# Turning a unit's maxima in the middle of the next burst, with rows that go through memory

## The chip, the cores and the metric

The kernel runs on one core of a Trainium2 chip. The metric is the device time of one execution in microseconds (us). The engines are PE (TensorE: matmuls; the profile lists its weight loads apart, as PEld), DVE (VectorE), ACT (ScalarE), POOL (GpSimd) and SP (SyncE, which issues nearly all DMAs here). Each engine runs its own instructions in order.

## The reference

Input x has 2048 rows (tokens) and 640 columns. The result mixes two branches with one gate per token:

```python
g = sigmoid((x * gate_w).sum(-1, keepdims=True))
a = softmax(q @ k.T * 20**-0.5) @ v     # 32 heads of 20, q, k, v = x @ wqkv
y = Cr @ (x @ Dr.T) - Ci @ (x @ Di.T)   # Fourier transform over hidden and tokens, real part
out = g * (a @ wo) + (1 - g) * y
```

All is in fp32. The softmax needs the maximum of each row of scores; that maximum is what the change is about.

## The kernel before, in words

**Projections.** Ahead of the main loop the kernel projects x to q, k and v (`qk_tile`, `v_pair`) and stores them to memory. Among the last q and k tiles stand ten *segments* (`segment`, `FILL`): in each, some steps of scores for maxima (`s_step`) alternate with the matmuls of one tile of the hidden Fourier transform (`hid_tile`). `FILL[4] = (0, 8, 7, 0)` means: a step and 0 pairs of the tile's matmuls, a step and 8, a step and 7, a step and 0. `HEAD` is the number of segments, `LEAD` the number of score steps done ahead of the loop: 10 x 4 and one more.

**Units and their two kinds of scores.** Attention goes by 32 units (a pair of heads times one half of the query tokens), each of 32 steps. Scores are computed twice. An *m* (`s_mm`, L171) multiplies 128 queries with 512 keys, and DVE reduces the tile to one maximum per query (L173). An *e* (L880) computes transposed scores, keys by queries, and ACT takes the exponential out of PSUM (L886). In the e, two extra rows of the q stack (rows `KROWS` and `KROWS + 1` of each half of the partitions) hold the negated maximum, split into two fp32r parts, and the k stack has ones there: the matmul subtracts the maximum. So all maxima of a unit have to be in these rows before its first e. The m's run `LEAD` steps ahead of the e's.

**From maxima to rows.** `max_nm` (L187) reduces a unit's 64 partial maxima per partition to 16 (2 heads x 8 query tiles), negated: nm, 128 x 16. `max_chain` turns nm with a PE transpose into 16 x 128 in a PSUM bank (L205), splits it on DVE into m1 and m2 (L115, L116), and four DMAs on SP copy them, 8 partitions each, into the four rows of the q stack (L213, L214).

**The main loop.** It is written out by hand as a string per cycle of 4 steps, `ORDER = "emFemFFFFemFeFFmeFFemFFFmmFFmeeB"`: 8 e's, 8 m's, 15 places for fills F (matmuls of the Fourier transform, later of the output projection; L614, L363, L685) and one burst B. From cycle `late` on there are no m's and the string is `LATE`. In a burst, `max_nm` runs first for a unit whose last m is done; then come reads of finished fill tiles (`run_extras`) and two AV steps (`av_step`, L533), each of four fp32 matmuls in the four 32-column quarters of the array, which add exp(scores) @ v; after them `max_chain`. The scores, the turn and the projections take PSUM banks in rotation from five (`bank`); a bank is free when its last reader is done.

**SP's order.** `at_step(i, fn)` puts a DMA into SP's program at the beginning of step i; SP issues in this order as early as what it waits for allows. The rows of a unit are placed two steps behind the turn. On the same queue are the loads of the Fourier matrices (in_cdft), of partial results (a_scr), the stores and loads of the softmax sums (l_scr, r_scr), and the loads of the next pair of heads (qk_scr).

**The lines to follow.** `FILL` and `LEAD` near the top, `s_end`, `max_nm` and `max_chain` (L175 to L219), the loop over `order` that calls `segment` (L438 to L453), and `burst` (L892 to L904).

Of the kernel before, what the change touches and what calls it, by code (L numbers as in the profile page):

```python
# [10 lines left out]
F32 = mybir.dt.float32  # L11
R = mybir.dt.float32r
AF = mybir.ActivationFunctionType
ALU = mybir.AluOpType
AX = mybir.AxisListType
# [3 lines left out]
P = 128  # L19
# [9 lines left out]
KROWS = 3 * DH  # L29
NU = 2 * NP  # L30
# [7 lines left out]
FIRST = {"e": (0, 0, 1, 1), "m": (1, 1, 1, 1)}  # L38


LEAD = 41


FILL = {4: (0, 8, 7, 0)}
HEAD = 10


# [23 lines left out]
def f32(ap):  # L71
    return ap.bitcast(F32)
# [3 lines left out]
def mix_kernel(ctx: ExitStack, tc: tile.TileContext, xa, wqk, wb, cdft, wo, out):  # L76
    nc = tc.nc
    pe, act, dve, pool, sp = nc.tensor, nc.scalar, nc.vector, nc.gpsimd, nc.sync
    ctx.enter_context(tc.manual_schedule())

    def pools(**kw):
        return ctx.enter_context(tc.tile_pool(**kw))

    const = pools(name="const", bufs=1)
    small = pools(name="small", bufs=1)
    work = pools(name="work", bufs=1)
    dram = pools(name="dram", bufs=1, space=DRAM)
# [8 lines left out]
    r_scr = dram.tile([NU, 4, 512], F32, name="r_scr")  # L96
    l_scr = dram.tile([NU, 4, 512], F32, name="l_scr")
    o_scr = dram.tile([D, S], F32, name="o_scr")

    ident = const.tile([P, P], F32, name="ident")  # L100
    make_identity(nc, ident)
# [9 lines left out]
    def split(dst1, dst2, src, e1, e2):  # L111
        if e1 is act:
            act.activation(dst1, src, AF.Copy)  # L113
        else:
            e1.tensor_copy(dst1, src)  # L115
        e2.tensor_tensor(dst2, src, f32(dst1), op=ALU.subtract)  # L116
# [8 lines left out]
    def bank():  # L125
        return ps_w.tile([P, 512], F32, name=f"ps{next(turn) % 5}")
# [23 lines left out]
    def q_unit(n):  # L150
        u = n % 2 * (S // 2)
        return qst[n // 2 % 2][:, u : u + S // 2]

    mx, nms, ends = {}, {}, []
    now, later = [-1], {}

    def at_step(i, fn):
        later.setdefault(i, []).append(fn)
# [16 lines left out]
    def s_end(i):  # L175
        n, s = divmod(i, 32)
        if n < NU and s == 31:
            if now[0] < 0:
                max_nm(n)
            else:  # L180
                ends.append(n)
        if s == 1 and 0 < n <= NU and now[0] < 0:
            max_chain(n - 1)

    def max_nm(n):
        nms[n] = small.tile([P, 16], F32, name="nm", bufs=2)
        dve.tensor_reduce(nms[n], mx.pop(n).rearrange("p h q c -> p (h q) c"), axis=AX.X, op=ALU.max, negate=True)  # L187

    def s_step(i):
        for fn in [s_mm(i, h) for h in range(2)]:  # L190
# [8 lines left out]
        return yp[z]  # L199


    def max_chain(n):
        q = q_unit(n)
        pt = bank()[:16, :P]
        pe.transpose(pt, nms.pop(n), ident)  # L205
        m1 = small.tile([16, P], R, name="m1")
        m2 = small.tile([16, P], R, name="m2")
        split(m1, m2, pt, dve, dve)

        def rows():  # L210
            for h in range(2):
                b = 64 * h + KROWS
                sp.dma_start(f32(q[b : b + 1, :]), f32(m1[8 * h : 8 * h + 8, :]))  # L213
                sp.dma_start(f32(q[b + 1 : b + 2, :]), f32(m2[8 * h : 8 * h + 8, :]))  # L214

        if now[0] < 0:
            rows()
        else:
            at_step(now[0] + 2, rows)  # L219


    pa = pools(name="att", bufs=1)
# [73 lines left out]
    stores, halves, hid_done = [], [], 0  # L296

    def flush(keep=0):
        while len(stores) > keep:
            sp.dma_start(*stores.pop(0))  # L300

    def qk_tile(c, t):
        w = wt[c]
        ps = bank()
        x1, x2 = xs[0][t], xs[1][t]
        for d in range(ND):
            if (c, t) == (0, 0) and d > 0:
                if d == 1:
                    idle(3)
                pe.matmul(ps, w[:, 0, d], x1[:, d], start=False, stop=False)  # L310
                pe.matmul(ps, w[:, 1, d], x1[:, d], start=False, stop=False)
                pe.matmul(ps, w[:, 0, d], x2[:, d], start=False, stop=d == ND - 1)
            else:
                three(ps, w[:, 0, d], w[:, 1, d], x1[:, d], x2[:, d], d == 0, d == ND - 1)
        if hid_done:
            if not halves:
                raw = pair_tile()
                halves.extend((raw[:, 1], raw[:, 0]))
            raw = halves.pop()
            act.activation(raw, ps, AF.Copy)  # L320
        st = pair_tile()
        st1, st2 = st[:, 0].bitcast(R), st[:, 1].bitcast(R)
        if hid_done:
            split(st1, st2, raw, pool, pool)
        else:
            split(st1, st2, ps, act, dve)
        stores.append((qk_scr[:, t, c * P : (c + 1) * P].rearrange("z p c -> p z c"), st))
        flush(1 if hid_done else 2)
# [24 lines left out]
    def hid_tile(i, read_out):  # L353
        j, st = divmod(i, NS)
        hf, ri = divmod(j, 2)
        new_y(0), new_y(1)
        w = wt["b", 2 + j]
        t, cs = st // 4, slice(st % 4 * P, (st % 4 + 1) * P)
        for d in range(ND):
            for z, (xz, wz) in enumerate(((0, 0), (0, 1), (1, 0))):  # L360
                for h in range(2):
                    r = slice(64 * h, 64 * h + 64)
                    pe.matmul(yp[h][:, :HE], xs[xz][t][r, d, cs], w[r, wz, d, :HE],  # L363
                              start=d == 0 and z == 0, stop=d == ND - 1 and z == 2)
                if (d, z) != (ND - 1, 2):
                    yield
        a = raw_tile()[:, :HE]
        y0, y1 = yp[0][:, :HE], yp[1][:, :HE]

        def read():  # L370
            act.activation(a, y0, AF.Copy, scale=-1.0 if ri else 1.0)  # L371
            dve.tensor_tensor(a, a, y1, op=ALU.subtract if ri else ALU.add)  # L372

        read_out(read, (a_scr[ri, hf, st], a))
        yield


    def segment(i, steps):
        def read_out(read, args):
            read()  # L380
            stores.append(args)

        tile_ = hid_tile(i, read_out)
        for n in FILL[steps]:
            run_s(step + 1)
            for _ in range(n):
                next(tile_)
# [3 lines left out]
    def run_s(upto):  # L391
        nonlocal step
        while step < upto:
            s_step(step)
            step += 1
# [27 lines left out]
    def load_v(p):  # L423
        vts[p] = v_tile()
        sp.dma_start(vts[p], v_scr[p])
# [12 lines left out]
    for n, c in enumerate(order):  # L438
        for t in range(4):
            m = 4 * n + t  # L440
            if m % 3 == 0 and hid_done < HEAD:
                segment(hid_done, 4)
                hid_done += 1
            qk_tile(c, t)
            if m == 8:
                load_v(0)
            if t == 1:
                if n + 1 < len(order):
                    fin()
                if n + 2 < len(order):  # L450
                    fin = load_wqk(order[n + 2])
    run_s(LEAD)
    flush()  # L453
# [73 lines left out]
    def av_step(i, n, kt):  # L527
        v = vts[n // 2]
        pp = [pts.pop((n, kt, qc)) for qc in range(2)]
        for qc in range(2):  # L530
            for h in range(2):
                j = 2 * qc + h
                pe.matmul(av[32 * j : 32 * j + DH + 1, :], v[:, kt, h * (DH + 1) : (h + 1) * (DH + 1)],  # L533
                          pp[qc][:, h, :], start=kt == 0, stop=kt == NS - 1)
        if kt == NS - 1:
            unit_end(i, n)
# [136 lines left out]
    def out_tile(tt, hf):  # L673
# [18 lines left out]
        def read():  # L692
            if now[0] < total - LEAD:
                act.activation(m, y0, AF.Copy, scale=g)
            else:
                dve.tensor_scalar(m, y0, g, 1.0, op0=ALU.mult, op1=ALU.mult)
            dve.scalar_tensor_tensor(m, y1, g, m, op0=ALU.mult, op1=ALU.add)
# [84 lines left out]
    start = 4 * HID  # L782
# [5 lines left out]
    for u in range(UNITS):  # L788
        k, t = LONG[u // HT], u % HT
# [3 lines left out]
    for u in range(2 * len(PRE)):  # L793
        n = 2 if u >= 2 * len(PRE) - SLOW else 1
# [3 lines left out]
    assert cycles[-1][1] <= last + 1  # L798
    late = -(-(total - LEAD) // 4)
    at_goal = 0  # L800
# [7 lines left out]
    for k, tt in enumerate(PRE):  # L808
        i = 4 * tiles[2 * k]

        def load(tt=tt, i=i):
            at_step(i - 6, load_pre(tt))
# [41 lines left out]

    heads = {"e": 0, "m": 2 * LEAD}

    held = []

    def score(kind):
# [5 lines left out]
        if kind == "m" or i <= 4 * late:  # L865
            h ^= FIRST[kind][(i - (LEAD if kind == "m" else 0) - 1) % 4]
        if kind == "m":
# [6 lines left out]
        if i < total:  # L874
# [14 lines left out]

            held.append(exp) if hold else exp()  # L890

    def burst(c):  # L892
        for n in ends:
            max_nm(n)
        run_extras(max(done - HIDS, 0) // 3, 2)
        for kt in (2 * c, 2 * c + 1):
            av_step(now[0], kt // NS, kt % NS)
            while held:
                held.pop(0)()
        while ends:  # L900
            max_chain(ends.pop(0))
        if c == HID - 1:
            start_dft()

# [58 lines left out]
    sel, o, rb = chain  # L963
# [80 lines left out]
```

## Time and profile before

| | us |
|---|---|
| median of 3 runs | 1880.69 (1880.5 to 1881.56) |
| the profiled execution | 1881.58 |
| its span, first to last instruction | 1879.7 |

The granted clock of PE was 1.000 in the profiled execution. In the profile's lines, a row of the timeline gives the start in us from the span's start, the time it covers, the engine, the line of the kernel, the operation, what is written and read, and the number of instructions that were merged. A row of waits gives the engine and line that waited, what it waited for, the total in us, the number of times and the longest. A row for one line or tile gives the shortest, median and longest duration in ns, and the first and last start. A row of windows gives the window, its length, the busy time and count of PE and then of PEld, the granted clock, the DMA share and GB/s.

### The profile page before, as it was taken

Reading aid. Unit: us, or ns where it says so; the run is one execution under the profiler, and the core shown is the slowest. Engines: PE = TensorE matmul, PEld = TensorE weight load, DVE = VectorE, ACT = ScalarE, POOL = GpSimd, SP = SyncE. Lnnn points to the kernel's source line nnn. Section 1 sums busy time; section 2 is a strip of 40 time slices with the busy share of each in tenths; the row PEclk is TensorE's granted clock in tenths of the full one; section 3 lists DMA queues with packets and bytes.
Section 4 is the critical chain, followed back from the end, with each engine's and each line's share of the span. In section 5 each row is a group of like instructions: output and inputs, shape, how many; then the busy total and the mean of one; then the engine's idle time right before and its main releaser. Section 6 shows DMA issues by size and latency. Waiting matters only on the chain. (4 is left out here: it accounts for less than half of the span.)

```text
span 1879.7 us, 44556 instructions
## 1 busy us (share of the span) xinstructions
PE 1870.3 (99%) x17453; PEld 1355.1 (72%) x17453; DVE 1446.3 (77%) x2404; ACT 1224.5 (65%) x2359; POOL 1075.1 (57%) x942
## 2 busy tenths in 40 slices
PE   9999999999999999999999999999999999999998
PEld 8988777777776767767677776776767777676666
DVE  4143469989898888888888888888888888889953
ACT  4221147777777767767676676766767667677785
POOL 1234421010045896566799899778789988634334
PEclk9999999999999999999999999999999999999999
DMA  7843341312325473536566576546476746342214
GB/s 233 180 137 141 134 140 48 80 59 66 115 69 185 147 230 125 162 123 189 194 182 226 173 241 197 167 131 188 162 234 197 213 152 202 112 111 68 62 36 159
DMA packets 174597, 280.51 MB, mean 149 GB/s; under 512 B 44095, under 2 KB 106687, under 8 KB 174387
## 3 DMA queue, kind: packets, MB, share of 16 engines
q1 hardware_dynamic: 173427, 275.69, 48.1%
q0 software_dynamic: 960, 1.97, 0.6%
q8 instruction: 137, 2.24, 0.5%
q14 instruction: 73, 0.60, 0.1%
HBM read 213.37 MB, written 63.52 MB: 147 GB/s over the span
## 5 line engine op out<-in xcount | busy, mean ns | idle before, releaser
L173 DVE TENSOR_REDUCE mx<-ps 128x1 f32<-128x512 f32 x2048 | 1296.1, 684 | 219.6 <-PE ps L171 199.6
L886 ACT ACTIVATE p<-ps 128x512 f32<-128x512 f32 x2048 | 1087.9, 598 | 429.3 <-PE ps L171 228.7
L171 PE MATMUL ps<-kst,qst 60*128 60x512 f32 x2048 | 776.5, 413 | 1.5 <-DVE mx L173 1.4
L880 PE MATMUL ps<-qst,kst 62*128 62x512 f32 x2048 | 698.4, 414 | 0.1
L614 PE MATMUL yp<-x,part 64*128 64x320 f32 x5376 | 645.8, 307 | 0.0
L614 PEld LDWEIGHTS yp<-x,part 64*128 64x128 f32 x5376 | 580.7, 186 | 7.2
L533 PE MATMUL av<-p,v 128*21 128x512 f32 x4096 | 490.6, 596 | 0.0
L880 PEld LDWEIGHTS ps<-qst,kst 62*128 62x128 f32 x2048 | 334.8, 184 | 202.5 <-DVE mx L173 182.2
L171 PEld LDWEIGHTS ps<-kst,qst 60*128 60x128 f32 x2048 | 368.2, 184 | 15.0 <-issue 3.8
L116 POOL TENSOR_TENSOR part<-raw,part 128x1024 fp32r<-128x1024 f32 (+1 forms) x129 | 290.3, 2251 | 10.3
L533 PEld LDWEIGHTS av<-p,v 128*21 128x21 f32 x4096 | 98.1, 100 | 225.8 <-issue 225.1
L363 PE MATMUL yp<-wb,x 64*128 64x320 f32 x1920 | 227.7, 307 | 0.3 <-ACT raw L371 0.2
L115 POOL CAST part<-raw 128x1024 fp32r<-128x1024 f32 (+1 forms) x129 | 127.1, 985 | 166.6 <-PE yp L614 155.3
L363 PEld LDWEIGHTS yp<-wb,x 64*128 64x128 f32 x1920 | 202.4, 186 | 5.2 <-DVE raw L372 0.8
L494 POOL TENSOR_TENSOR raw<-raw,raw 128x1024 f32<-128x1024 f32 x77 | 185.5, 2410 | 24.6 <-DMA raw<-in_cdft 23.7
L563 POOL TENSOR_TENSOR o<-o,rb 128x512 f32<-128x512 f32 x31 | 40.2, 1296 | 145.8 <-DMA rb<-r_scr 94.5
L119 PE MATMUL ps<-x,part 128*128 128x512 f32 (+1 forms) x236 | 90.7, 384 | 0.3
L685 PE MATMUL yp<-x,part 64*128 64x320 f32 x720 | 90.9, 310 | 0.0
L121 PE MATMUL ps<-x,part 128*128 128x512 f32 (+1 forms) x236 | 89.6, 380 | 0.1
L120 PE MATMUL ps<-x,part 128*128 128x512 f32 (+1 forms) x236 | 89.1, 377 | 0.0
L116 POOL TENSOR_TENSOR x<-araw,x 128x320 fp32r<-128x320 f32 x96 | 83.8, 873 | 7.7
L320 ACT ACTIVATE p<-ps 128x512 f32<-128x512 f32 x32 | 19.1, 598 | 93.8 <-PE ps L121 93.8
(85 smaller groups left out, 1142.2 us busy)
## 6 DMA issues: line engine op xcount, KB each, us to landing
raw<-in_cdft SPq DMA_DIRECT2D x192, 512.0 KB
araw<-a_scr SPq DMA_DIRECT2D x176, 160.0 KB
qk_scr<-p SPq DMA_DIRECT2D x40, 512.0 KB
kst<-qk_scr SPq DMA_DIRECT2D x90, 160.0 KB
qst<-qk_scr SPq DMA_DIRECT2D x90, 160.0 KB
a_scr<-raw SPq DMA_DIRECT2D x64, 160.0 KB
yt<-y_scr SPq DMA_DIRECT2D x64, 160.0 KB
y_scr<-yt SPq DMA_DIRECT2D x64, 160.0 KB
```

What stands on the lines that cost most here:

```text
L115: e1.tensor_copy(dst1, src)
L116: e2.tensor_tensor(dst2, src, f32(dst1), op=ALU.subtract)
L119: pe.matmul(ps, st1, mv1, start=first, stop=False)
L171: pe.matmul(ps, q[b : b + KROWS, qt * P : (qt + 1) * P], k[b : b + KROWS, kc * 512 : (kc + 1) * 512], start=True, stop=True)
L173: return lambda: dve.tensor_reduce(mx[n][:, h, qt, kc : kc + 1], ps, axis=AX.X, op=ALU.max)
L363: pe.matmul(yp[h][:, :HE], xs[xz][t][r, d, cs], w[r, wz, d, :HE], start=d == 0 and z == 0, stop=d == ND - 1 and z == 2)
L494: pool.tensor_tensor(raws[0], raws[0], raws[1], op=ALU.add if PRODUCTS[n][0][1][0] > 0 else ALU.subtract)
L533: pe.matmul(av[32 * j : 32 * j + DH + 1, :], v[:, kt, h * (DH + 1) : (h + 1) * (DH + 1)], pp[qc][:, h, :], start=kt == 0, stop=kt == NS - 1)
L614: pe.matmul(yp[h][:, :HE], c[r, cz, cs], a[r, az], start=s == 0 and z == 0, stop=s == NS - 1 and z == 2)
L685: pe.matmul(yp[h][:, :HE], o[r, oz, d], wos[d, hf][r, wz], start=d == 0 and z == 0, stop=d == ND - 2 and z == 2)
L880: pe.matmul(pt, k[b : b + KROWS + 2, kt * P : (kt + 1) * P], q[b : b + KROWS + 2, qc * 512 : (qc + 1) * 512], start=True, stop=True)
L886: act.activation(pts[n, kt, qc][:, h], pt, AF.Exp, scale=float(DH) ** -0.5)
```

## The change

The maxima of a unit are no longer turned at the end of the burst that made nm, but one burst later, between its two AV steps. The turn is no transpose but four fp32 matmuls, each of nm (now 128 x 32: the 16 columns twice) against 32 columns of the identity, into the four 32-partition quarters of a bank. The result, 128 x 32, is split into one tile of two parts, which a DMA stores to memory one step later; two steps after that, four DMAs load the rows from there in pieces of 32 numbers. LEAD goes from 41 to 43: the fifth and the ninth segment do five steps instead of four.

```diff
-LEAD = 41
-FILL = {4: (0, 8, 7, 0)}
+LEAD = 43
+FILL = {4: (0, 8, 7, 0), 5: (0, 6, 5, 4, 0)}
...
+    m_scr = dram.tile([NU, P, 2, 32], F32, name="m_scr")
...
         if s == 1 and 0 < n <= NU and now[0] < 0:
-            max_chain(n - 1)
+            turn_max(n - 1)
 
     def max_nm(n):
-        nms[n] = small.tile([P, 16], F32, name="nm", bufs=2)
-        dve.tensor_reduce(nms[n], mx.pop(n).rearrange("p h q c -> p (h q) c"), axis=AX.X, op=ALU.max, negate=True)
+        nms[n] = small.tile([P, 32], F32, name="nm", bufs=2)
+        m = mx.pop(n).rearrange("p h q (o c) -> p o (h q) c", o=1).to_broadcast([P, 2, 16, 4])
+        dve.tensor_reduce(nms[n].rearrange("p (o k) -> p o k", o=2), m, axis=AX.X, op=ALU.max, negate=True)
...
-    def max_chain(n):
+    def turn_max(n):
         q = q_unit(n)
-        pt = bank()[:16, :P]
-        pe.transpose(pt, nms.pop(n), ident)
-        m1 = small.tile([16, P], R, name="m1")
-        m2 = small.tile([16, P], R, name="m2")
-        split(m1, m2, pt, dve, dve)
-
-        def rows():
+        pt = bank()[:, :32]
+        nm = nms.pop(n)
+        for j in range(4):
+            c = slice(32 * j, 32 * j + 32)
+            pe.matmul(pt[c, :], nm, ident[:, c], start=True, stop=True)
+        m = small.tile([P, 2, 32], R, name="m")
+        split(m[:, 0], m[:, 1], pt, dve, dve)
+
+        def store():
+            sp.dma_start(m_scr[n], f32(m))
+
+        def load():
             for h in range(2):
-                b = 64 * h + KROWS
-                sp.dma_start(f32(q[b : b + 1, :]), f32(m1[8 * h : 8 * h + 8, :]))
-                sp.dma_start(f32(q[b + 1 : b + 2, :]), f32(m2[8 * h : 8 * h + 8, :]))
+                for z in range(2):
+                    b = 64 * h + KROWS + z
+                    sp.dma_start(f32(q[b : b + 1, :]).rearrange("o (k j c) -> o k j c", j=4, c=32),
+                                 m_scr[n, :, z].rearrange("(o j k) c -> o k j c", o=1, j=4)[:, 8 * h : 8 * h + 8])
 
         if now[0] < 0:
-            rows()
+            store()
+            load()
         else:
-            at_step(now[0] + 2, rows)
+            at_step(now[0] + 1, store)
+            at_step(now[0] + 3, load)
...
-                segment(hid_done, 4)
+                segment(hid_done, 5 if hid_done in (4, 8) else 4)
...
+    turned = []
+
     def burst(c):
         for n in ends:
             max_nm(n)
         run_extras(max(done - HIDS, 0) // 3, 2)
         for kt in (2 * c, 2 * c + 1):
             av_step(now[0], kt // NS, kt % NS)
+            while turned:
+                turn_max(turned.pop(0))
             while held:
                 held.pop(0)()
-        while ends:
-            max_chain(ends.pop(0))
+        turned[:] = ends
+        ends.clear()
```

## The prediction

> **What bounds the kernel now.** I read the page's span and engine shares first, then the waits of TensorE (PE), then PE's timeline around the place that the diff touches.
>
> ```profile
> span 1879.7 us, 44556 instructions
> PE 1870.3 (99%) x17453; PEld 1355.1 (72%) x17453; DVE 1446.3 (77%) x2404; ACT 1224.5 (65%) x2359; POOL 1075.1 (57%) x942
> ```
>
> ```profile
> PE ps L265 <- DVE x L259: 1.5, 1, 1.5
> PE ps L171 <- DVE mx L173: 1.4, 2, 0.7
> PE ps L310 <- ACT x L113: 0.7, 1, 0.7
> PE yp L363 <- ACT raw L371: 0.2, 1, 0.2
> ```
>
> PE is busy for 99% of the span, and all the gaps of its matmul records come to 3.8 us. So the order in which PE is fed is the time: an edit counts by what it adds to or takes from PE's stream. The ends of matmuls are modelled, so I take costs from starts. The next fence is PE's timeline: a burst that ends with a turn of maxima, and the next one, without.
>
> ```profile
> 1001.49 1.91 PE L533 MATMUL av<-p,v 128*21 128x512 f32 x16
> 1003.33 0.28 PE L205 MATMUL ps<-ident,nm 128*16 128x128 f32 x1
> 1003.54 0.50 PE L880 MATMUL ps<-qst,kst 62*128 62x512 f32 x1
> ...
> 1008.00 1.91 PE L533 MATMUL av<-p,v 128*21 128x512 f32 x16
> 1009.85 0.49 PE L880 MATMUL ps<-qst,kst 62*128 62x512 f32 x1
> ```
>
> From the burst's first AV matmul to the first score matmul behind it: 2.05 us with the turn (1003.54 - 1001.49), 1.85 without (1009.85 - 1008.00). More closely, the turn occupies PE from 1003.33 to 1003.54, **0.207 us** by the starts in ns. Nothing else hides it: it is PE's own time. The row of the tile nm says that all 32 turns are alike:
>
> ```profile
> L205 PE MATMUL ps<-ident,nm x32: 276/277/278, 220.3 to 1809.6; 128*16 128x128 f32 x32
> ```
>
> One of them (220.3) lies before the main loop, 31 in it: 31 x 0.207 = 6.4 us, 0.34% of the time, is all that this part can ever win.
>
> **What the new turn costs (x).** Four fp32 matmuls of 32 columns in the four column quarters, between the two AV steps of a burst. AV's own shape tells how such matmuls run:
>
> ```profile
> 1008.00 0.14 PEld L533 LDWEIGHTS av<-p,v 128*21 128x21 f32 x8 [0.28 <-issue]
> 1008.45 0.12 PEld L533 LDWEIGHTS av<-p,v 128*21 128x21 f32 x4 [0.31 <-issue]
> 1008.88 0.12 PEld L533 LDWEIGHTS av<-p,v 128*21 128x21 f32 x4 [0.31 <-issue]
> ```
>
> ```profile
> L533 PEld LDWEIGHTS av<-p,v x4096: 96/101/102, 261.4 to 1854.2; 128*21 128x21 f32 x196
> L533 PE MATMUL av<-p,v x4096: 592/592/609, 261.4 to 1854.6; 128*21 128x512 f32 x196
> ```
>
> The code has 512 AV steps of 4 matmuls, 2048; the trace has 4096, so one fp32 matmul runs as two passes. A burst is four rounds of four concurrent passes, 0.43 us apart (1008.88 - 1008.45): 0.84 ns per moving column. The new turn is eight passes, two more rounds, of 32 columns: 2 x 0.027 = 0.054 us if their weight loads are hidden as AV's are. The burst's first round, whose loads nothing hides, lasts 0.45 instead of 0.43: an exposed load costs about 0.015. With one exposed load (the second round's, behind a round too short to cover it) **x = 0.07 us**, my value. Below 0.054 I see no way, since columns must stream. From above: both loads wholly exposed, 2 x 0.10, is 0.20; each round waiting for its results, as priced in the third rival, 0.38. I take the low end because the shape, the tile and the engine state are AV's own.
>
> The Trainium skill, page "TensorEngine Tiling (Array Packing)", Key Properties, says that a change of tiling mode drains TensorE and that column tiles load and multiply independently; by it a turn in AV's own quarters needs no drain. Its page "TensorE: Matmul & The Clock Gate", "Wait — 56ns, not 53.3ns?", speaks against the change: matmul starts are never closer than about 25 ns. By that rule eight passes would cost an estimated 8 x 25 = 0.20 us, and nothing would be won.
>
> The trace has passes closer than that where they go to different quarters; in this view of AV's instructions four matmuls begin within 0.04 us:
>
> ```profile
> 1001.48:1001.52 0.04, 0.03 (x4) 0.04 (x7) 1.00 0.38 69
> ```
>
> **Does the new turn wait?** PE executes in order, so a wait there holds the second AV step and all behind it. Two things must be ready at T + 0.87 (T: start of the burst's AV): nm and a bank.
>
> ```profile
> 999.42 3.27 DVE L173 TENSOR_REDUCE mx<-ps 128x1 f32<-128x512 f32 x5
> 1002.60 0.21 DVE L187 TENSOR_REDUCE nm<-mx 128x16 f32<-128x64 f32 x1
> 1003.65 0.28 DVE L115 CAST m<-ps 16x128 fp32r<-16x128 f32 x1 [0.83 <-PE ps L205]
> 1003.96 0.28 DVE L116 TENSOR_TENSOR m<-ps,m 16x128 fp32r<-16x128 f32 x1
> ```
>
> nm was made at T + 1.1 of the same burst; with a lead of 43 the unit's last maxima fall one burst earlier (two steps sooner, and they then end exactly with a cycle), so nm is a burst old. The bank is that of the third-last m before the burst; the five reduces run 0.60 apart and end at 1002.69 (T + 1.20), so the third-last ended at T + 0.0. Neither waits. VectorE (DVE): nm reads 128 elements instead of 64, by L173 against L187 (684 against 209 ns for 512 against 64) 0.07 us more, and the split's two operations shrink from 128 to 32 elements a partition. DVE waits for PE beside it; off the path, zero either way. Gain in the loop: 31 x (0.207 - 0.07) = **-4.25 us**.
>
> **The rows through memory.** Now the four row DMAs start 0.6 us behind the turn; score matmuls of the unit begin two cycles later:
>
> ```profile
> 1003.95 0.68 SPq L213 DMA_DIRECT2D qst<-m  x1
> ...
> 1006.10 0.64 SPq L214 DMA_DIRECT2D qst<-m  x1
> ```
>
> ```profile
> 1013.93 0.45 PE L880 MATMUL ps<-qst,kst 62*128 62x512 f32 x2
> ```
>
> ```profile
> 712.35 0.54 SPq L547 DMA_DIRECT2D l_scr<-o  x1
> 714.39 0.33 SPq L550 DMA_DIRECT2D lc<-l_scr  x1
> ```
>
> The first score of the unit is due at T + 12.4. After: turn's results T + 1.1, split (two operations, at most 0.28 each) T + 1.7, store. The load waits on SP for the store to land; the same kind of pair, l_scr and lc, stands 2.04 us apart: T + 3.75. Four loads 0.7 apart: the last is issued at T + 5.9 and, with another 2.04, usable at T + 7.9. That leaves 4.5 us, so the round trip costs PE nothing. Behind the waiting load on SP stand loads of araw, in_cdft and rb: delayed by some 1.1 us once a unit, and PE's list of waits above has no DMA in it at all. If this cover were gone, each microsecond late would cost 31 us in all. The only landing that the page gives is that of far larger loads:
>
> ```profile
> kst<-qk_scr POOLq DMA_DIRECT2D x6, 160.0 KB, 6.2
> ```
>
> With 6.2 for both landings the rows would come at T + 16.2, too late; those move 160 KB each, the change 32 KB out and four times 4 KB back, so I stay with the 8 KB pair.
>
> **The lead.** Two more score steps are done ahead of the loop, in the fifth and ninth segment, and the last cycle with m's loses four. Each moved step costs PE the same where PE is the limit; but a segment is not. PE's timeline of the fifth segment, and DVE's:
>
> ```profile
> 162.80 0.72 PE L171 MATMUL ps<-kst,qst 60*128 60x512 f32 x4
> 163.36 1.34 PE L363 MATMUL yp<-wb,x 64*128 64x320 f32 x16
> 164.54 0.40 PE L171 MATMUL ps<-kst,qst 60*128 60x512 f32 x2
> 164.78 1.19 PE L363 MATMUL yp<-wb,x 64*128 64x320 f32 x14
> 165.81 0.40 PE L171 MATMUL ps<-kst,qst 60*128 60x512 f32 x2
> 166.14 0.50 PE L119 MATMUL ps<-x,part 128*128 128x512 f32 x1
> ```
>
> ```profile
> 163.33 3.68 DVE L173 TENSOR_REDUCE mx<-ps 128x1 f32<-128x512 f32 x6 [5.21 <-PE ps L171]
> ```
>
> Now the tile behind the segment starts 3.34 us after it began. There are five banks; that tile takes the ninth, so it needs the fourth reduce, done at 163.33 + 0.68 + 3 x 0.60 = 165.81: no wait. With five steps it takes the eleventh and needs the sixth reduce, done at 163.33 + 3.68 = 167.01, or 4.21 behind the start, plus about 0.05 for the signal: 4.26 - 3.34 = 0.92 us later. DVE, not PE, sets this. The extra step's own PE time is 0.24 (164.78 - 164.54), the lower end. Two segments: **+1.8** (at least +0.5). At the other end of the loop:
>
> ```profile
> 1796.21:1802.39 6.18, 3.07 (x8) 1.39 (x8) 1.00 0.02 4
> 1802.39:1807.78 5.39, 1.71 (x4) 0.66 (x4) 1.00 0.00 0
> ```
>
> Cycle by cycle with its m's: dropping from 8 to 4 saved 0.79. Those four stood late in the cycle, some alone; the four that go now mostly run beside an e, on the other half of the rows. I take **-0.3** (between 0 and -0.79). The unit turned ahead of the loop: zero, its drain stays. One store and its wait on SP there delay the stores of q and k by about 2 us once: zero.
>
> Sum: -4.25 + 1.8 - 0.3 = -2.75 us. The profiled execution took 1881.58 us, 1.9 more than its span and 0.9 above the median 1880.69; the difference goes onto the median: **1877.9 us**. The case by itself, with x from 0.054 to 0.12 and the lead from +0.2 to +1.9: 1876.1 to 1879.9.
>
> **Rivals.** *The lead is almost free* (the extra step's reduces find their banks, so +0.2): -4.25 + 0.2 = -4.05, 1876.6 us. For it: DVE idles 5.21 us ahead of the segment; against it: five banks and the 0.60 of a reduce.
>
> *The loads show*: x = 0.20, the turn wins 0.2 and the lead stays: +1.3, 1882.0 us. For it: a load takes 0.10 and a 27 ns round cannot cover it; against it: the first round of a burst shows only 0.015 of it.
>
> *Each short round pays its latency* (ends slower): a pass lasts 0.592 by its row, 0.16 beyond its 0.43 of streaming. If the second pass, which adds onto the first one's result, waits for it, and the next AV round likewise, each round is 0.027 + 0.16: x = 0.38, 31 x 0.17 + 1.5 = +6.9, 1887.6 us. Place: between the AV steps. It turns the sum positive from x = 0.16 and makes it over 0.2% slower from x = 0.28. Against it: AV and the projections add passes onto the same bank closer than their latency (0.43 against 0.592; none in the trace so close as 0.03).
>
> *The rows come late*: 1 us behind 12.4 in each unit is +31, about 1909 us. It needs the two landings to sum to over 8.5 us instead of 4.1. The Trainium skill, "DMA: Bandwidth & Descriptors", Specifications, wants 512 B a piece for full rate and a read-modify-write below; the rows come in 128 B pieces, which no row here prices.
>
> **Numbers.** Forecast 0.42, lead free 0.22, loads show 0.15, latency 0.12, rows late 0.05, some other stall 0.04. A change of 0.2%, 3.8 us, is about what a measurement of this kernel can tell from none. Faster by that (below 1876.9): the free lead, and about a third of the forecast's chance: 0.37. Slower (above 1884.5): latency, rows and other: 0.21. Between: 0.42. The range runs from 1875.5 to 1887.8: it takes in all but late rows and other stalls, with 0.6 below the lowest case for the scatter of the runs.
>
> **What would show it.** Right: the first score starts 1.92 us after a unit burst's AV (now 2.05); the second AV step of such a burst starts 0.07 later than in others; PE's waits list no DMA; the fifth segment lasts about 4.3 us. Wrong: a unit burst of 2.05 or over (loads, latency); a PE wait on qst from m_scr (rows); segments as long as before (lead free).

## The result and the profile after

The changed kernel takes **1875.5 us** (median of 6 runs, 1874.5 to 1876.81); the kernel before took 1881.12 beside it (6 runs, 1880.5 to 1883.11). The ratio is 0.997, with a 95% interval from 0.996 to 0.998: faster by 5.6 us, where 2.75 were forecast. The time lies at the lower edge of the range. The direction was right; one term of the sum, forecast as a cost, was none, and one was missing. The granted clock is 0.998 to 1.0 in every profile below but that of the changed kernel with the old lead (0.988), and 1.00 in every stage whose row is shown.

The page after, as before PE without gaps:

```profile
span 1872.7 us, 45009 instructions
PE 1864.0 (100%) x17677; PEld 1354.8 (72%) x17677; DVE 1444.5 (77%) x2404; ACT 1223.2 (65%) x2359; POOL 1076.1 (57%) x942
```

```profile
PE ps L275 <- DVE x L269: 1.5, 1, 1.5
PE ps L172 <- DVE mx L174: 1.4, 2, 0.7
```

The second fence is the whole list of PE's waits. Of the four waits before, two are gone. One (0.7 us, on ACT) lies 8 us behind the start, ahead of everything that is compared below. The other, on ACT's raw (0.2 us in that list), will turn out to be the thread to one part of the gain. Now PE's timeline at a burst with a turn:

```profile
999.25 1.06 PE L543 MATMUL av<-p,v 128*21 128x512 f32 x8
1000.12 0.24 PE L210 MATMUL ps<-ident,nm 128*32 128x32 f32 x8
1000.18 1.04 PE L543 MATMUL av<-p,v 128*21 128x512 f32 x8
1001.16 0.49 PE L890 MATMUL ps<-qst,kst 62*128 62x512 f32 x1
```

The second AV step starts 0.06 us behind the turn's start, and the first score 1.91 us behind the burst's start (1001.16 - 999.25); before it was 2.05, and 1.85 without a turn. The weight loads of the turn:

```profile
999.70 0.13 PEld L210 LDWEIGHTS ps<-ident,nm 128*32 128x32 f32 x4 [0.31 <-issue]
1000.12 0.13 PEld L210 LDWEIGHTS ps<-ident,nm 128*32 128x32 f32 x4 [0.30 <-issue]
```

The first four run under the AV round ahead of the turn. By their starts in ns the eight passes begin at 1000124, 131, 137, 143 and 152, 159, 165, 172, AV's next at 1000183: two rounds 0.028 to 0.031 apart, so the second load does not show either. All 32 turns are alike:

```profile
L210 PE MATMUL ps<-ident,nm x256: 192/196/218, 220.4 to 1802.0; 128*32 128x32 f32 x128
```

The rows of this unit go through memory on SP, and its first score follows:

```profile
1000.89 0.32 SPq L215 DMA_DIRECT2D m_scr<-m  x1
1003.18 2.75 SPq L221 DMA_DIRECT2D qst<-m_scr  x4
```

```profile
1011.56 0.42 PE L890 MATMUL ps<-qst,kst 62*128 62x512 f32 x2
```

Issues end at T + 6.7 (1003.18 + 2.75 - 999.25); the score comes at T + 12.3. The fifth segment has become longer, as the bank count said:

```profile
162.28 0.74 PE L172 MATMUL ps<-kst,qst 60*128 60x512 f32 x4
...
165.95 0.50 PE L172 MATMUL ps<-kst,qst 60*128 60x512 f32 x1
166.55 0.50 PE L120 MATMUL ps<-x,part 128*128 128x512 f32 x1
```

```profile
166.55 0.19 PEld L120 LDWEIGHTS ps<-x,part 128*128 128x128 f32 x1 [0.41 <-DVE mx L174]
```

It lasts 4.27 us (166.55 - 162.28), before 3.34. The last fence is the weight load of the tile behind it: it waits for one of DVE's reduces, as the bank count has it.

**Where the time came from.** The starts of the segments and of the AV bursts cut the run into stages. Rows of the windows view of before, with length, then busy time and count of PE, PEld, DVE, ACT and POOL, granted clock, DMA share and GB/s: from the first segment to the first burst; the cycle behind burst 50; the Fourier stage (bursts 54 to 222); two cycles near the loop's end.

```profile
105.88:261.43 155.55, 153.85 (x915) 124.22 (x914) 67.28 (x112) 33.74 (x60) 64.53 (x64) 1.00 0.39 138
575.72:582.87 7.15, 6.88 (x64) 4.62 (x62) 5.64 (x10) 4.85 (x9) 5.41 (x3) 1.00 0.61 149
601.94:1667.42 1065.48, 1065.48 (x10768) 757.38 (x10766) 894.42 (x1485) 745.47 (x1421) 845.12 (x677) 1.00 0.58 177
1802.38:1807.78 5.40, 5.40 (x54) 3.52 (x53) 4.64 (x10) 4.44 (x9) 3.10 (x4) 1.00 0.00 0
1807.78:1813.25 5.47, 5.44 (x53) 3.06 (x51) 1.90 (x5) 4.07 (x9) 0.99 (x2) 1.00 0.01 3
```

The same of after:

```profile
105.36:262.44 157.08, 155.17 (x925) 125.29 (x924) 69.35 (x115) 33.76 (x60) 64.62 (x64) 1.00 0.38 137
576.20:582.45 6.25, 6.25 (x64) 4.47 (x63) 5.57 (x10) 4.57 (x9) 4.19 (x3) 1.00 0.74 197
601.36:1661.85 1060.49, 1060.49 (x10914) 755.81 (x10913) 894.05 (x1485) 745.25 (x1421) 845.88 (x677) 1.00 0.60 179
1796.32:1801.12 4.80, 4.80 (x49) 3.04 (x49) 2.17 (x6) 3.84 (x8) 2.48 (x3) 1.00 0.01 3
1801.12:1806.16 5.04, 5.04 (x60) 3.15 (x58) 1.67 (x5) 4.21 (x10) 1.62 (x3) 1.00 0.03 7
```

The stage ahead of the loop costs 1.53 more, as forecast in sign; everything else is shorter, the Fourier stage by 4.99. The start of the first segment moves by up to 3.2 us between executions of these kernels (105.11 to 108.30: loads at the start), so profiles are compared from there on: 1773.85 us before (1879.73 - 105.88), 1767.35 after, **-6.50**. A second profile of each, below, gives -6.40.

### The profile page after: what moved, and what is told of

Its sections match the earlier page's. It is cut to its first block, busy times and chain, and to the rows that moved or that the text cites. A ratio compares the mean times of both kernels' runs of the same rounds, so it can differ in the third digit from the quotient of the medians.

```text
span 1872.7 us, 45009 instructions
## 1 busy us (share of the span) xinstructions
PE 1864.0 (100%) x17677; PEld 1354.8 (72%) x17677; DVE 1444.5 (77%) x2404; ACT 1223.2 (65%) x2359; POOL 1076.1 (57%) x942
```

## The experiments

My theory after the result: the turn has about the forecast price, and the lead of 43 is not a loss. The rival: the lead costs what was forecast, and the turn, or its place, gains more than PE's own time at it. A third came up with the traces: ordinary cycles, without a turn, had become shorter too, and what the diff changes in them is where the operands lie. (m and nm together take 640 bytes a partition less than m1, m2 and nm did, and the tiles allocated behind them slide down.)

**The lead alone** (before, with the first two edits of the diff and five steps in the fifth and ninth segment; the old transpose at the old place).

```diff
-LEAD = 41
-FILL = {4: (0, 8, 7, 0)}
+LEAD = 43
+FILL = {4: (0, 8, 7, 0), 5: (0, 6, 5, 4, 0)}
...
-                segment(hid_done, 4)
+                segment(hid_done, 5 if hid_done in (4, 8) else 4)
```

> The kernel before with the lead of 43 alone (two segments of five steps); the old transpose stays at the end of the burst that made nm. Theory 1 (the lead only costs): two segments longer by 0.92 and 0.76 us, cycle 245 shorter by 0.6: +1.1 us against before, and the other cycles as in before (median 6.307 us). Theory 2 (the lead also wins in the loop, because a unit's last m now falls at a cycle's end): the other cycles lose some 2.5 to 3.3 us, so -1.4 to -2.2 us against before, with the cycle in which a pair's first m stands down from 6.36 to 6.30.

1881.52 us, ratio 0.9993 to 1.0011: no cost that can be measured. By the profile:

```profile
105.11:262.55 157.44, 155.39 (x919) 125.22 (x918) 69.66 (x116) 33.75 (x60) 64.54 (x64) 1.00 0.39 136
576.54:582.80 6.26, 6.26 (x65) 4.55 (x63) 5.58 (x10) 4.66 (x9) 4.53 (x3) 1.00 0.58 174
601.82:1666.60 1064.78, 1064.78 (x10767) 757.05 (x10765) 896.00 (x1485) 745.38 (x1421) 844.87 (x677) 1.00 0.57 178
```

+1.89 ahead of the loop, as forecast, but -0.89 in the one cycle behind burst 50, -0.70 in the Fourier stage and -0.97 behind it. What vanished behind burst 50 shows in before's rows of one PE load, what it waits for, and what that waits for:

```profile
578.23 0.18 PEld L363 LDWEIGHTS yp<-wb,x 64*128 64x128 f32 x1 [0.47 <-ACT raw L371]
```

```profile
577.74 0.44 ACT L371 ACTIVATE raw<-yp 128x320 f32<-128x320 f32 x1 [0.87 <-POOL raw L494]
```

```profile
575.33 2.37 POOL L494 TENSOR_TENSOR raw<-raw 128x1024 f32<-128x1024 f32 x1 [2.93 <-DMA raw<-in_cdft]
```

and in the lead-only kernel:

```profile
575.25 2.38 POOL L494 TENSOR_TENSOR raw<-raw 128x1024 f32<-128x1024 f32 x1 [2.01 <-DMA raw<-in_cdft]
```

The fill ahead can only be read out by ACT when POOL is done, POOL waits for a load, and PE waits for ACT. Both kernels issue the load 8.5 us ahead of burst 50 (at 567.27 and 568.05 on SP); POOL begins 0.39 us ahead of the burst in before (575.72 - 575.33) and 1.29 ahead in this one (576.54 - 575.25). The load lands 0.9 us sooner and the wait is gone. Why it does was not settled. The wait belongs to the lead and not to one execution: this cycle lasts 6.78 to 7.50 us in the six profiles of kernels with the old turn and the lead of 41, and 6.23 to 6.49 in the ten with the lead of 43.

**The old transpose in the new place** (lead 43, rows direct; max_chain is called behind the first AV step of the next burst).

```diff
             av_step(now[0], kt // NS, kt % NS)
+            while turned:
+                max_chain(turned.pop(0))
...
-        while ends:
-            max_chain(ends.pop(0))
+        turned[:] = ends
+        ends.clear()
```

> Lead of 43 and the turn between the two AV steps of the next burst, but as the old 16x128 transpose with rows straight from SBUF. If the form of the turn matters (a transpose leaves the column quarters and PE drains twice): a unit burst of 2.05 + 0.1 = 2.15 us to the next score against 1.85 in others, about +3 us against the lead alone. If only the place matters (nm is a burst old, nothing else): 1.91 us as in the changed kernel, -4.2 us against the lead alone.

1885.89 us, ratio 1.0014 to 1.0032: slower. Its burst with a turn:

```profile
1004.32 1.06 PE L533 MATMUL av<-p,v 128*21 128x512 f32 x8
1005.30 0.28 PE L205 MATMUL ps<-ident,nm 128*16 128x128 f32 x1
1005.51 1.06 PE L533 MATMUL av<-p,v 128*21 128x512 f32 x8
1006.50 0.49 PE L880 MATMUL ps<-qst,kst 62*128 62x512 f32 x1
```

2.18 us to the next score: the transpose costs 0.335 here, against 0.207 behind the burst. 31 x 0.128 = 4.0, and the medians are 4.4 apart. So the place by itself is no gain; for the old transpose it is a loss.

**The quarters at the end of the burst** (after, with the call behind the second AV step).

```diff
-            while turned:
-                turn_max(turned.pop(0))
...
+        while turned:
+            turn_max(turned.pop(0))
```

> The changed kernel with its four matmuls behind the second AV step of that burst instead of between the two. If the form of the turn is what wins: 1.91 us from a unit burst's first AV matmul to the next score, time within 1 us of the changed kernel. If the middle of the burst is needed: about 2.05 us, +4 us against the changed kernel.

1875.33 us, ratio 0.9959 to 0.9981.

```profile
1000.29 1.92 PE L543 MATMUL av<-p,v 128*21 128x512 f32 x16
1002.02 0.25 PE L210 MATMUL ps<-ident,nm 128*32 128x32 f32 x8
1002.19 0.50 PE L890 MATMUL ps<-qst,kst 62*128 62x512 f32 x1
```

1.90 us: the same as in the middle. What pays is the shape, not the place. The shape changed in several things at once: at AV's 0.84 ns per column, 128 columns would by themselves take an estimated 0.107 of the old 0.207 us, and how the rest divides into the weight load and a change between the two ways of using the array was not separated.

**The turn three times** (each of its matmuls; the result is that of the last).

```diff
-        for j in range(4):
...
+        for k in range(3):
+            for j in range(4):
...
```

> The changed kernel with each of the turn's four matmuls issued three times into the same place: 16 passes more a unit. If a round of four short passes costs its streaming and its share of a load (0.03 us): +0.12 us a unit, +3.8 us in all, a unit burst of 2.03 us. If each round pays the latency of a pass (0.19 us): +0.76 us a unit, +23 us.

1881.03 us, ratio 0.999 to 1.0008, 5.5 above after.

```profile
1002.03 1.06 PE L544 MATMUL av<-p,v 128*21 128x512 f32 x8
1002.90 0.37 PE L211 MATMUL ps<-ident,nm 128*32 128x32 f32 x24
1003.09 1.08 PE L544 MATMUL av<-p,v 128*21 128x512 f32 x8
1004.10 0.50 PE L891 MATMUL ps<-qst,kst 62*128 62x512 f32 x1
```

2.07 us to the score, 0.164 more for four more rounds: 0.041 a round, close to streaming. 31 x 0.164 = 5.1 of the 5.5. The turn is priced.

**Moving the tiles.** An unused tile of 640 bytes a partition puts after's large tiles back where before has them; one of 384 bytes moves before's; the lead-only kernel also got one of 384.

```diff
+    pad = small.tile([P, 160], F32, name="pad")
```

> The changed kernel with 640 unused bytes a partition ahead of the small tiles, so that every large tile (x, part, p, raw, v) lies where it lay before the change. Theory 3 (layout: the smaller turn tiles let all large tiles slide down by 640 bytes a partition, and cycles without a turn became 0.011 us shorter by that): those cycles go back from 6.295 to 6.306 us, +2.7 us, 1878.2. Rival (rows by way of memory or the form of the turn shorten all cycles): 6.295 us stays, 1875.5.

> The kernel before with 384 unused bytes ahead of the small tiles: large tiles then lie, in steps of 1024 bytes, as in the changed kernel. Theory 3, if a period of 1024 bytes or a divisor counts: cycles without a turn 6.295 us instead of 6.306, -2.7 us against before, turns still 0.207. Rival, or a longer period: 6.306 us, time of before.

> The lead of 43 and the 384 unused bytes, with the old turn: all of the change's side effects without its turn. If the terms add up (lead about 0, layout -1.0): 1.0 us under before, cycles of the Fourier stage without a turn 6.30 on a trimmed mean, cycle 51 without its wait of 0.9 us, turns 0.207; what is left to the changed kernel is then its turn, -4.2. If layout and lead only seemed to win by scatter: time of before, 6.309.

After with 640: 1876.38 us, ratio 0.9967 to 0.9986. Before with 384: 1880.08, ratio 0.9987 to 1.0005. Lead with 384: 1880.55, ratio 0.9989 to 1.0007. By time alone no difference between these and the kernels without the tile can be told. The stages of the profiles show one; the Fourier stage of after with 640, and of before with 384:

```profile
604.02:1665.41 1061.39, 1061.39 (x10914) 756.63 (x10912) 894.58 (x1485) 745.18 (x1421) 844.80 (x677) 1.00 0.58 179
```

```profile
602.42:1666.51 1064.09, 1064.09 (x10768) 755.45 (x10766) 894.25 (x1485) 745.28 (x1421) 845.39 (x677) 1.00 0.57 177
```

0.90 longer than after, 1.39 shorter than before, with the same instructions. The table further down has the cycles.

**After with the old lead.**

```diff
-LEAD = 43
+LEAD = 41
...
-                segment(hid_done, 5 if hid_done in (4, 8) else 4)
+                segment(hid_done, 4)
```

> The changed kernel with the lead of 41 and ten segments of four steps: a unit's last maxima fall inside the next cycle, so nm, turn and rows all come one cycle (6.3 us) later against the same first score. If the rows arrive 7.9 us behind the turn's burst as predicted, the first score (due 6.1 us behind it) waits about 1.8 us in each of 31 units: +56 us less 1.1 for the lead, about 1930 us. If the round trip is so short that the old lead would do (under 6.1 us): about 1874.4. If the rows take 12 us, they were all but late with the lead of 43: +180 us.

1964.89 us, ratio 1.0427 to 1.0465. The turn falls a burst later, and the rows come too late in every unit; PE's waits, and a score of one unit, whose turn stands in the burst at 1044.08:

```profile
PE ps L890 <- DMA qst<-m_scr: 59.0, 32, 3.7
```

```profile
1045.72 0.34 SPq L215 DMA_DIRECT2D m_scr<-m  x1
1047.66 2.75 SPq L221 DMA_DIRECT2D qst<-m_scr  x4
```

```profile
1051.79 0.59 PE L890 MATMUL ps<-qst,kst 62*128 62x512 f32 x2 [1.50 <-DMA qst<-m_scr]
```

This is the only kernel in which the arrival of the rows can be seen: here at T + 7.7, in the median of the units at T + 8.05 (5.9 to 10.0). It is 89 us above after; 59.0 of them are this wait. The granted clock is 0.988 here, and 0.986 to 0.991 in its four runs, against 0.998 to 1.0 in the other profiles: an estimated 1.2% of 1962.6 us, some 23, may go with that. Why the clock is lower in this kernel alone no run shows.

**The two extra steps by themselves** (after; ten segments of four, and one step alone behind the q and k tiles 16 and 22, so that its reduces find free banks).

```diff
-                segment(hid_done, 5 if hid_done in (4, 8) else 4)
+                segment(hid_done, 4)
...
+            if m in (16, 22):
+                run_s(step + 1)
```

> The changed kernel with the two extra score steps out of the segments and alone between two tiles of q and k (behind the tiles 16 and 22 of 32), where DVE idles. If the longer segments cost 0.92 and 0.76 us because the sixth reduce frees the bank late: a step alone costs its PE time, 0.24 to 0.34, so -1.0 us against the changed kernel, segments all 3.35 long again (or as long as before). If the steps cost the same anywhere: no change.

1875.32 us, ratio 0.9956 to 0.9981. From the first segment's start to the last one's it is 0.64 shorter (234.87 - 105.80 against 235.07 - 105.36), where 1.0 was expected. The fifth segment is back at 3.35, but over before (128.00) the two steps still cost 1.07 there, against 1.71 in after. So only a third of the price goes with the place, and a step alone costs more than its 0.24 of PE's time. A gain of this size does not show in the time.

**The same again.** After and before once more, and before with 256 bytes.

> The changed kernel once more, for a second profile and more times: turns 0.061, Fourier cycles 6.30, cycle 51 at 6.25 us if these belong to the kernel and not to one execution; 5.6 us under before, between 4.5 and 6.5.

> The kernel before once more, for a second profile: if the wait of 0.9 us in cycle 51 and the cycles of 6.309 us belong to the kernel, both come again; if they are of one execution, cycle 51 is 6.25 and the cycles scatter.

> The kernel before with 256 unused bytes, so another place of the large tiles again. If the place counts at a finer step than 1024 bytes, the trimmed mean of the Fourier cycles without a turn leaves 6.309 (down to 6.30 or up); if only the one shift of the change helps, it stays at 6.309.

After again: 1875.14 us, ratio 0.9955 to 0.9979; its profile from the first segment on has 1767.25 us (1873.51 - 106.26). Before again: 1883.24 in a single run, of which 1773.65 from the first segment on (1881.42 - 107.77); the cycle behind burst 50 again holds the wait (7.44 us), and that of after again does not (6.25). Before with 256: 1881.43 in a single run, with ordinary cycles as in before.

**Which tile.** Before, with 384 bytes ahead of x alone; and before with the Fourier stage's work tiles (part, p, raw, v) moved by 384 and x by 1024.

```diff
+    pad2 = pa.tile([P, 96], F32, name="pad2")
```

> The kernel before with 384 unused bytes ahead of x alone (and of what lies above it), the tiles part, p, raw and v in their old place. If the place of the streamed operand counts: the trimmed mean of the Fourier cycles without a turn 6.300 instead of 6.309, the stage from burst 54 to burst 222 (1065.4) some 1.3 us shorter. If that of part, p, raw and v counts: 6.309 and 1065.4.

> The kernel before with part, p, raw and v 384 bytes higher and x 1024 bytes higher. If the place of part, p, raw and v counts: 6.300, the stage some 1.3 us shorter. If that of x counts, with a period of 1024 bytes: 6.309 and 1065.4. If both are 6.309, the two have to move together.

1884.2 and 1886.55 us in a single run each, before beside them 1881.84. Neither expectation held: neither layout brings the gain, and both profiles are longer, from the first segment on by 2.1 and 4.3 us. The Fourier stage of each, and three of the q and k tiles between two segments:

```profile
603.81:1670.07 1066.26, 1066.26 (x10768) 757.83 (x10766) 894.18 (x1485) 745.68 (x1421) 843.37 (x677) 1.00 0.57 177
123.94:134.63 10.69, 10.68 (x45) 8.38 (x45) 2.74 (x5) 1.40 (x3) 3.80 (x4) 1.00 0.30 113
```

```profile
603.96:1672.41 1068.45, 1068.45 (x10768) 757.50 (x10766) 894.53 (x1485) 744.80 (x1421) 843.31 (x677) 1.00 0.57 177
124.05:134.74 10.69, 10.69 (x46) 8.39 (x47) 2.73 (x5) 1.36 (x3) 3.80 (x4) 1.00 0.30 113
```

The starts of these projection matmuls stand 233 ns apart on average in both kernels, and 229 in before: it is the pace of the matmuls themselves that differs, not a wait.

**Whole multiples of 2048.** After with two unused tiles, so that work tiles, x and what follows begin there.

```diff
+    pad = small.tile([P, 48], F32, name="pad")
...
+    pad2 = pa.tile([P, 176], F32, name="pad2")
```

> The kernel after, with two unused tiles so that the Fourier work tiles, x and the tiles behind it begin at whole multiples of 2048 bytes in a partition. Program and operands are else the same. If the pace of PE depends on how the start of an operand lies within such a block, whole multiples should be the best case: cycles of the Fourier stage below 6.300 us (6.300 after, 6.309 before, 6.328 in the slowest layout), below 10.51 us for three q and k tiles, and a time of 1872 to 1875 us. If it depends on how the tiles lie to each other, or on something else, the time is that of after (1875.5) or up to 4 us above it, as where x and the work tiles were moved apart.

1874.83 us, ratio 0.9955 to 0.998: not told from after.

```profile
600.30:1661.85 1061.55, 1061.55 (x10914) 757.11 (x10912) 893.95 (x1485) 744.75 (x1421) 844.12 (x677) 1.00 0.58 178
123.09:133.52 10.43, 10.43 (x45) 8.37 (x46) 2.74 (x5) 1.29 (x3) 3.81 (x4) 1.00 0.30 116
```

The projections are the fastest seen (227 ns from start to start), the ordinary cycles of the Fourier stage are about as slow as before's. So whole multiples are not the best case everywhere, and that expectation held in one stage and failed in the other. The layouts side by side (ordinary cycle: between two bursts of the Fourier stage, no turn, without the ten longest and the ten shortest; three tiles: from the end of the first segment to the second; another choice of which cycles next to a turn to leave out moves a mean by up to 0.002 us):

| tiles moved, against before | kernels | us per ordinary cycle | three q and k tiles, us |
|---|---|---|---|
| none | before, before again, lead alone, old transpose in the new place | 6.309 (all four) | 10.51 |
| none | after with 640 | 6.307 | 10.51 |
| +256 | before with 256 | 6.309 | 10.51 |
| +384 | before with 384, lead with 384 | 6.299, 6.301 | 10.52 in the first |
| -640 | after, after again, quarters at the end, thrice, steps by themselves | 6.301, 6.300, 6.302, 6.301, 6.295 | 10.52 in after |
| x +384 alone | one | 6.313 | 10.69 |
| work tiles +384, x +1024 | one | 6.328 | 10.69 |
| whole multiples of 2048 | one | 6.308 | 10.43 |

## Why the prediction was right in its direction and wrong in its size

The stages put the terms apart. The lead is the lead-only kernel less before; the turn is after with 640 less the lead-only kernel, both with the large tiles where before has them; the addresses are after less after with 640:

| stage, us | lead | turn and rows | addresses | all |
|---|---|---|---|---|
| first segment to first burst | +1.89 | -0.36 | 0.00 | +1.53 |
| bursts 0 to 54 | -1.24 | -0.63 | +0.29 | -1.58 |
| bursts 54 to 222 | -0.70 | -3.39 | -0.90 | -4.99 |
| bursts 222 to 248 | -0.97 | -0.49 | -0.05 | -1.51 |
| the rest | -0.03 | +0.01 | +0.08 | +0.06 |
| sum | **-1.05** | **-4.86** | **-0.58** | **-6.49** |
| forecast | +1.5 | -4.25 | none | -2.75 |

These are differences of single profiles; a second pair for the lead (lead with 384 less before with 384) gives +0.13 in all, after +0.8 in the rest of the run behind the loop, which was not followed. The timed medians of the lead are 0.1 apart, and the interval of the ratio goes from -1.3 to +2.1, so the time alone does not exclude +1.5; the stages put the lead between -1 and about 0.

- **The turn: right.** x was to be 0.07 us; it is 0.061 (1.906 - 1.845 in the medians of all bursts), and 31 x (0.207 - 0.061) = 4.5. Another 0.17 came from the turn ahead of the loop, forecast at zero (ninth segment 4.59 instead of 4.76), and 0.18 from the first cycle, which was not followed. Of the rivals, *each short round pays its latency* (0.38) and *the loads show* (0.20) are out, by after's rows and by the turn done thrice. The Trainium skill, page "TensorE: Matmul & The Clock Gate", "Wait — 56ns, not 53.3ns?", has starts at least about 25 ns apart; passes in different quarters start 6 to 7 ns apart here, so the rule does not reach across quarters, and its 0.20 did not come.
- **The shape is the cause, not the place**, shown by the two crossed kernels. The prediction's premise, that a turn in AV's own quarters runs like AV, holds in the middle and at the end. The Trainium skill, page "TensorEngine Tiling (Array Packing)", Key Properties, has a change of tiling mode drain TensorE; the old transpose, not in quarters, fits that, with 0.128 us more between two quarter steps than behind them. No run here shows the drain itself.
- **The rows: right.** Forecast usable at T + 7.9, seen at T + 8.05 in the median with the old lead; needed at T + 12.3. The cover of over 4 us is real and it is what the lead of 43 buys: with 41 it is gone, at 59 us of waits and 89 in all. The rival *the rows come late* was true of that kernel and not of this one.
- **The segments: right.** +0.92 for the fifth as worked out, by the sixth reduce; the ninth grew by 0.93 in the lead-only kernel (3.83 to 4.76). The *lead almost free* rival had this mechanism wrong, though its time, 1876.6, came nearer: that was other gains, not free banks.
- **The step that failed: the lead's price behind the segments.** The prediction set -0.3 for the loop's end and nothing for the loop itself; the lead alone measured -0.97 at the end and -1.94 in the loop ahead of it, so the +1.8 of the segments, which came as +1.89, was paid back (-0.97, -1.51 and +1.82 in the second pair). At the end, the last cycle with m's went from 5.40 to 4.80, -0.60, within its bound of 0.79; the cycle behind it lost 0.43, of which 0.15 is the turn, and the rest was not followed. In the loop, a wait of 0.9 us behind burst 50 vanished, and further 0.35 and 0.70 in small pieces: cycles in which a new pair of heads starts lose some 0.06 each (6.356 in before to 6.295 in after, in the median). The prediction had quoted the row of that wait, at 0.2 us, and passed it over. PE's row counted only what PE's matmul waited; its weight load waited 0.47, and the cycle was 0.9 over its neighbours. Nor did it ask which rows of a list of waits the two added steps would shift.
- **What was not in the sum: the addresses.** Smaller turn tiles move every large tile by 640 bytes. The same program then runs its ordinary cycles at 6.300 instead of 6.309 us: some -0.6 to -0.9 here, -1.0 for before with 384 alone. That the position changes PE's pace is shown by the profiles of kernels that differ in nothing else, most plainly by the 227 to 233 ns between the same projection matmuls; for the smaller gain in the Fourier stage it rests on 0.01 us a cycle, though the means of the two groups do not overlap in any profile. How the position does it is open. Moving x alone by 384 does not bring the gain, nor does moving the work tiles by 384 where x moves by 1024, and alignment to 2048 helps one stage and not the other.

With -4.9, about -1 to 0 and -0.6 to -0.9 the sum is -5.5 to -6.8; timed were -5.6 and, in the repetition, about -6. No version beats after by more than can be measured: the steps by themselves and the aligned tiles are within 0.7 us of it.

## What to carry to other kernels

Here a small matmul among matmuls in array quarters paid by being in quarters too; whether it then stood between them or behind them made no difference, while the old transpose was dearer between them than behind them. When work is moved ahead of a loop, price what it does to every wait in the list, by the length of the cycle and not by the wait's own row, and not only the place that it moves to. A change of tile sizes moves the tiles behind it, which was worth -1.0 to +4.3 us here, so an effect of that size is not its own until a kernel with the same addresses has been run.

## What the runs showed of the hardware

- PE's pace depends on where the operands lie in their partition: 6.295 to 6.328 us for the same 8 scores, 8 m's, fills and burst, and 10.43 to 10.69 us for the same three projection tiles (227 to 233 ns from one matmul's start to the next) at a granted clock of 1.0.
- Passes of 32 fp32 columns in four quarters cost 0.03 us a round of four, at most 0.041 when repeated, and their weight loads of 0.11 us are hidden under the round ahead.
- Writing 32 KB and reading 16 KB of it back in pieces of 32 numbers takes about 6 us on one queue: store issued at T + 1.6, rows usable at T + 7.7 in the unit shown, of which the four loads' issues fill 2.75.
